# Splitting the last product's output over two PSUM banks, two loads made of three, and one zero product fewer, in a decode kernel of attention and MLP

## The chip, the cores and the metric

The kernel runs on one core of one Trainium2 chip. The metric is the device time of one execution in microseconds (us). Six executions of the kernel before in the first comparison took 661.54 to 661.99 us. With one core there is no second die to compare with; all runs told of here are of state fast. The span in a profile (660.1 us) runs from the first to the last instruction and is about 1.4 us shorter than the time.

## The reference

Four tokens (batch 4, one position each, model width 640) pass a pre-norm attention block over a cache of 4096 positions with 32 heads, and then a pre-norm MLP with mish activation. Shapes and the part that matters:

```python
q = (layernorm(x) @ wq)                      # 640 -> 32 heads x 128
p = softmax(q . k_cache * 128**-0.5)         # k_cache 4 x 32 x 4096 x 128, bf16
h = x + (p . v_cache) @ wo                   # wo 4096 x 640
a = mish(layernorm(h) @ w1 + b1)             # w1 640 x 1728
out = h + a @ w2                             # w2 1728 x 640, out 4 x 1 x 640, bf16
```

The two caches are 268 MB of the 283 MB that are read. The change concerns the last few microseconds, `a @ w2 + h`, and the load of `wo`.

## The kernel before

Each engine has its own program; `need` waits for marks that other engines set. SyncE issues nearly all loads into one queue, in order: the caches, then `wo`, `w1`, `w2`. `w2` (13 full blocks of 128 rows, and a tail of 64) is loaded in row groups of 5, 4, 3 and 1 blocks, each with its own semaphore. The parts that the change touches (cuts marked):

```python
# N = 4 tokens, D = 640, KO = 2 halves of OC = 320 columns, QD = 32, FS = [0, 5, 9, 12, 13]
y2_ps = red[:, 0:KO, 0:OC]           # half k: PSUM bank k, partitions 32k to 32k + 3
WOS = [(k, 0, G) for k in range(NHG - 1)] + [(NHG - 1, a, b) for a, b in ((0, 4), (4, 7), (7, G))]

def store(p, h):                     # one half each: SyncE half 0, ScalarE half 1
    p.need(("o_bf", h))
    load(p, out_rows[:, h * OC : (h + 1) * OC], o_bf[h * QD : h * QD + N, :], ("out", h), f"OUT{h}")
# ScalarE, last:
ac.need(("y2", 1))
ac.do(lambda: a.copy(out=o_bf[QD : QD + N, :], in_=y2_ps[QD : QD + N, 1, :]), ("o_bf", 1), "AC")
store(ac, 1)
# VectorE, last:
dv.need(("y2", 0))
dv.do(lambda: v.tensor_copy(out=o_bf[0:N, :], in_=y2_ps[0:N, 0, :]), ("o_bf", 0), DV)

# TensorE, tail (cut): busy(n) issues n zero products of 512 columns into a bank that nobody reads
for c in range(DC):                  # the residual h, as products with an identity
    for k in range(KO):
        mm(y2_ps[k * QD : k * QD + N, k, :].rearrange("b (m c) -> b c m", c=DC)[:, c, :],
           st[:, c, :], ident_f[:, k * P // KO : (k + 1) * P // KO], False, False)
busy(4)
pe.need("act")
def w2_mm(j):                        # one block of rows: two products, in two column groups of the array
    for k in range(KO):
        mm(y2_ps[k * QD : k * QD + N, k, :], act[0:rows, j, :], ...)   # 4 x 320
pe.need("w2t"); w2_mm(FM)
for j0, j1 in zip(FS, FS[1:]):
    if j0 == FS[2]:
        busy(3)
    pe.need(("w2", j0))
    for j in range(j0, j1):
        w2_mm(j)
```

The softmax here doesn't subtract the row's maximum and nothing guards it: scores larger than these inputs give would overflow.

## Time and profile before

| what | value | where it is read |
|---|---|---|
| time | 661.62 us, median of 3 | the runs |
| DMA share | 9 tenths or more in 39 of 40 slices | page, part 2 |
| bytes read, rate | 283.35 MB, 429 GB/s | page, part 3 |
| TensorE, VectorE busy | 59%, 62% | page, part 1 |
| last wait for w1 | until 651.13 us | chain of waits |

The page of the kernel before; in the second line the engines' busy time in us, and in the digits one tenth per digit for 40 equal slices of the span:

```profile
span 660.1 us, 4898 instructions
...
PE 391.0 (59%) x2604; PEld 68.8 (10%) x1631; DVE 407.8 (62%) x255; ACT 41.1 (6%) x158; POOL 1.8 (0%) x13
...
DMA  9999999999999999999999999999999999999997
...
HBM read 283.35 MB, written 0.01 MB: 429 GB/s over the span
```

The load stream is the clock of this kernel. The two busiest engines are idle for some 40% of the span, and what they do is free as long as it ends before the next piece of data lands. Only after the last loads have landed does every instruction count. The chain of waits shows where that begins (start in us, duration, what):

```profile
627.60 23.53 DMA slotB<-in_B_w_dram
...
651.18 1.28 PE red L722 x29
...
655.10 1.68 PE red L722 x20
656.78 0.32 PE o_ps L722
...
657.54 0.69 PE red L722 x8
658.22 0.47 DVE o_bf L718
```

The long line is the wait for w1, 23.53 us from issue to landing. The tail after it is a chain of 9 us. The timeline of its end (start, duration, engine, line, operation, output and inputs, count, and in brackets the idle time before it and what ended it; PEld is a weight load):

```profile
655.10 0.30 PE L722 MATMUL red<-w_tail,act 64*4 64x320 bf16 x2 [0.22 <-DVE act L711]
...
655.33 1.46 PE L722 MATMUL red<-slotA,act 128*4 128x320 bf16 x18
656.07 0.36 PEld L722 LDWEIGHTS red<-slotA,act 128*4 128x4 bf16 x8 [0.25 <-DMA slotA<-in_B_w_dram]
...
656.71 0.39 PE L722 MATMUL o_ps<-zeros,ident 128*128 128x512 bf16 x1
656.94 0.60 PE L732 MATMUL o_ps<-zeros,ident 128*128 128x512 bf16 x2
657.47 0.36 PEld L722 LDWEIGHTS red<-slotA,act 128*4 128x4 bf16 x8 [0.66 <-DMA slotA<-in_B_w_dram]
657.47 0.71 PE L722 MATMUL red<-slotA,act 128*4 128x320 bf16 x8
658.21 0.48 DVE L718 CAST o_bf<-red 4x320 bf16<-4x320 f32 x1 [3.17 <-PE red L722]
658.25 0.42 ACT L441 CAST o_bf<-red 4x320 bf16<-4x320 f32 x1 [4.46 <-PE red L722]
658.69 0.28 ACTq L262 DMA_DIRECT2D out_dram<-o_bf  x1
658.72 0.35 SPq L262 DMA_DIRECT2D out_dram<-o_bf  x1
```

TensorE starts w2's second row group at 656.07, on the landing of its load. The three zero products (o_ps) follow, and the third and fourth group start at 657.47. "DMA" is named as the releaser there, but the trace has that load landed at 657.18: the zero products held it up. Then come two casts side by side, one on each engine, and two stores.

### The profile page before, as it was taken

To read this page: it belongs to the slowest core of one execution; us is meant where nothing else is said; L and a number is where in the kernel's file an instruction comes from. 1 tells how busy PE (TensorE), PEld (TensorE's weight loads), DVE (VectorE), ACT (ScalarE), POOL (GpSimd) and SP (SyncE) were. 2 spreads that over 40 slices of the span, in tenths; PEclk is the share of its full clock that TensorE was granted. 3 is DMA by queue.
4 is the path that set the end of the run, shared out by engine and by line. 5 is a ranking of instruction groups with operands and counts; after the bars stand their busy time and mean duration, and the time that the engine had idled before them with its cause. 6 is when DMAs were issued, how large, how long until landed. Compare 5 with 4: busy or idle time off the path is not lost. (4 is left out here: it accounts for less than half of the span.)

```text
span 660.1 us, 4898 instructions
## 1 busy us (share of the span) xinstructions
PE 391.0 (59%) x2604; PEld 68.8 (10%) x1631; DVE 407.8 (62%) x255; ACT 41.1 (6%) x158; POOL 1.8 (0%) x13
## 2 busy tenths in 40 slices
PE   1365758456327595838307485828534757675878
PEld 0100100101101010101100010100110001010145
DVE  1078988295048778677219688848306798867612
ACT  0200000000000000000000000000000000000011
POOL 0000000000000000000000000000000000000000
PEclk9999787879659796869668678977965879786869
DMA  9999999999999999999999999999999999999997
GB/s 417 409 445 445 438 441 417 422 445 438 434 437 425 429 445 433 437 437 425 429 445 433 437 437 425 429 445 433 433 445 425 425 445 433 433 445 425 413 419 308
DMA packets 6883, 283.48 MB, mean 429 GB/s; under 512 B 781, under 2 KB 1113, under 8 KB 2138
## 3 DMA queue, kind: packets, MB, share of 16 engines
q1 hardware_dynamic: 6856, 283.35, 99.4%
q8 instruction: 6, 0.10, 0.1%
q14 instruction: 3, 0.02, 0.0%
q10 hardware_dynamic: 18, 0.01, 0.0%
HBM read 283.35 MB, written 0.01 MB: 429 GB/s over the span
## 5 line engine op out<-in xcount | busy, mean ns | idle before, releaser
L529 DVE TENSOR_TENSOR slotA<-slotA,q_bc 128x8192 bf16<-128x8192 bf16 x32 | 140.6, 4415 | 90.5 <-DMA slotA<-in_A_k_cache_dram 90.5
L529 DVE TENSOR_TENSOR slotB<-slotB,q_bc 128x8192 bf16<-128x8192 bf16 x32 | 140.7, 4416 | 16.5 <-DMA slotB<-in_A_k_cache_dram 16.5
L540 DVE TENSOR_REDUCE s_f<-red 128x64 f32<-128x1024 f32 x64 | 78.0, 1218 | 98.5 <-PE red L732 98.4
L732 PE MATMUL red<-slotA,ident 128*128 128x512 bf16 x480 | 137.5, 450 | 0.0
L732 PE MATMUL red<-slotB,ident 128*128 128x512 bf16 x480 | 127.3, 425 | 0.0
L722 PE MATMUL red<-slotA,ident 128*128 128x512 bf16 x32 | 14.2, 445 | 126.4 <-PEq L49 126.4
L722 PE MATMUL pv<-slotC,e 128*32 128x512 bf16 x768 | 53.1, 437 | 36.8 <-PEq L49 33.9
L722 PE MATMUL red<-slotB,ident 128*128 128x512 bf16 x32 | 14.1, 441 | 87.2 <-PEq L49 87.2
L402 ACT ACTIVATE ex<-s_f 128x64 bf16<-128x64 f32 x64 | 16.4, 256 | 512.0 <-DVE s_f L540 512.0
L554 DVE TENSOR_TENSOR e<-ex,hmask 128x512 bf16<-128x512 bf16 x64 | 39.8, 682 | 0.0
L722 PEld LDWEIGHTS pv<-slotC,e 128*32 128x32 bf16 x768 | 22.6, 108 | 95.7 <-issue 82.1
L722 PEld LDWEIGHTS red<-slotA,ident 128*128 128x128 bf16 x32 | 3.2, 99 | 195.1 <-issue 195.0
L722 PEld LDWEIGHTS red<-slotB,ident 128*128 128x128 bf16 x32 | 3.1, 98 | 169.2 <-issue 169.2
L722 PEld LDWEIGHTS o_ps<-pv_sb,selo 128*32 128x32 f32 x136 | 13.5, 109 | 65.1 <-issue 65.1
L722 PE MATMUL o_ps<-pv_sb,selo 128*32 128x128 f32 x136 | 18.0, 276 | 0.0
L722 PE MATMUL pv<-slotA,e 128*32 128x512 bf16 x256 | 14.5, 380 | 0.2 <-PEq L49 0.2
L412 ACT COPY pv_sb<-pv 128x512 f32<-128x512 f32 x16 | 9.4, 585 | 69.8 <-PE pv L722 69.8
L402 ACT ACTIVATION_READ_ACCUMULATOR ex<-s_f 128x1 f32 x64 | 11.9, 186 | 0.0
L722 PEld LDWEIGHTS pv<-slotA,e 128*32 128x32 bf16 x256 | 6.7, 97 | 23.4 <-issue 17.5
L519 DVE CAST b1T<-pv 128x13 bf16<-128x13 f32 x1 | 0.2, 173 | 14.0 <-PE pv L722 14.0
L579 DVE RECIPROCAL rl<-misc 32x1 f32<-32x1 f32 x4 | 0.6, 150 | 12.8 <-PE misc L722 12.8
L722 PE MATMUL red<-slotC,lnT 128*32 128x512 bf16 x40 | 4.5, 631 | 5.6 <-PEq L49 5.6
(105 smaller groups left out, 76.3 us busy)
## 6 DMA issues: line engine op xcount, KB each, us to landing
slotC<-in_A_v_cache_dram SPq DMA_DIRECT2D x2, 4096.0 KB, 39.0
slotC<-in_A_wq_dram SPq DMA_DIRECT2D x1, 5120.0 KB, 15.5
slotB<-in_A_wo_dram SPq DMA_DIRECT2D x3, 1280.0 KB, 15.6
slotB<-in_B_w_dram SPq DMA_DIRECT2D x2, 864.0 KB, 22.5
slotA<-in_B_w_dram SPq DMA_DIRECT2D x1, 800.0 KB, 18.5
slotB<-in_A_wo_dram SPq DMA_DIRECT2D x1, 640.0 KB, 19.3
slotA<-in_B_w_dram SPq DMA_DIRECT2D x1, 640.0 KB, 18.9
slotB<-in_A_wo_dram SPq DMA_DIRECT2D x1, 480.0 KB, 20.0
```

Of the source, the lines that this page charges most:

```text
L402: lambda: a.activation(out=ex[:, sl], in_=s_f[:, sl], func=ACT.Exp, scale=SCALE, accum_out=rs[:, b, s : s + 1],),
L412: lambda: a.copy(out=pv_sb[:, :, :].rearrange("p r d -> p (r d)"), in_=pv[:, :]),
L519: dv.do(lambda: v.tensor_copy(out=b1T[:, 0:FM], in_=b1_ps[:, 0:FM]), "b1m", DV)
L529: lambda: v.tensor_tensor(out=t, in0=t, in1=q_bc[:, hg, b, :].unsqueeze(1).to_broadcast([P, RS, Dh]), op=ALU.mult,),
L540: lambda: v.tensor_reduce(out=s_f[:, s * RS : (s + 1) * RS], in_=red[:, k : k + 2, :].rearrange("p k (r c) -> p (k r) c", c=CW), axis=AX.X ...
L554: lambda: v.tensor_tensor(out=e[:, sl, :], in0=ex[:, sl].unsqueeze(2).to_broadcast([P, RS, G]), in1=hmask[:, :].unsqueeze(1).to_broadcast( ...
L579: dv.do(lambda: v.reciprocal(out=rl[:, :], in_=l_ps), ("rl", hg), DV)
L722: lambda: nc.tensor.matmul(out_, lhsT=lhsT, rhs=rhs, start=start, stop=stop, skip_group_check=skip),
L732: return t.add_instruction(mybir.InstMatmult(name=nc.get_next_instruction_name(), engine=mybir.EngineType.PE, ins=[t.lower_ap(rhs), t.lowe ...
```

## The change

Its intent: each cast reads 160 columns instead of 320, so that both end sooner. For that each half is put in two banks, so that VectorE reads bank 0 and ScalarE bank 1 of both halves. (The Trainium skill, "PSUM — Partial Sum Buffer", section "PSUM bank collisions raise a hardware error", asks that two engines never be on one bank and quadrant at once; two banks keep to that.) As each half now comes from both engines, each store waits for both. Besides, one zero product goes, and wo's last row group is loaded in two parts, 5 and 3 rows per partition instead of 4, 3 and 1.

```diff
+    QC = OC // 2
+    y2_ps = red[:, 0:2, 0:QC]
-    ... for a, b in ((0, 4), (4, 7), (7, G))]
+    ... for a, b in ((0, 5), (5, G))]
     def store(p, h):
-        p.need(("o_bf", h))
+        p.need(("o_bf", 0), ("o_bf", 1))
-            a.copy(out=o_bf[QD : QD + N, :], in_=y2_ps[QD : QD + N, 1, :])
+            a.copy(out=o_bf[0 : QD + N, QC:OC], in_=y2_ps[0 : QD + N, 1, :])
-        v.tensor_copy(out=o_bf[0:N, :], in_=y2_ps[0:N, 0, :])
+        v.tensor_copy(out=o_bf[0 : QD + N, 0:QC], in_=y2_ps[0 : QD + N, 0, :])
-        for k, w in enumerate((OC, OC, 512, 512)):     # zeroing of the banks
+        for k, w in enumerate((QC, QC, 512, 512)):
     # residual: 20 products of 32 columns instead of 10 of 64 (cut)
     def w2_mm(j):
-            for k in range(KO): mm(y2_ps[k * QD : k * QD + N, k, :], ...)
+            last = j == FM - 1
+            order = [(h, q) for q in range(2) for h in range(KO)] if last else [
+                (h, q) for h in range(KO) for q in range(2)]
+            for h, q in order:         # half h, bank q, 160 columns
+                args = (y2_ps[h * QD : h * QD + N, q, :], act[0:rows, j, :], ...)
+                if last or q == 0: mm(*args)
+                else: mm_same(*args, tile=(rows, QD), place=(0, h * QD))   # no weight load
-                busy(3)
+                busy(2)
```

## The prediction

> **What bounds it now.** The page: DMA share 9 tenths in 39 of 40 slices, 429 GB/s, 283.35 MB in a span of 660.1 us; TensorE 59%, VectorE 62%. The kernel is a load stream with a short tail; the change touches only the tail.
>
> The chain of waits and the timeline give the tail. The second w1 part lands at 651.13 and TensorE starts on it at 651.18. w1 ends near 653.25, the activation at 655.05, w2 starts at 655.10. TensorE then waits for w2's second row group (landing 656.03, products from 656.07). They stream until 656.61, three zero products run 656.71 to 657.37, w2's third group starts at 657.47 although its data landed at 657.18. Products end at 658.18; VectorE casts 658.21 to 658.69 (479 ns), ScalarE 658.25 to 658.66 (416 ns); stores are issued at 658.69 and 658.72, and 1.37 us later the last lands.
>
> **What the change does, costed.**
> 1. One zero product fewer in the w2 tail: they step 0.22 us. The third group would start at 657.25; its landing (657.18 plus about 0.04) allows that, the last row (lands 657.57, wanted about 657.6) just about. Gain 0.2 us, on the chain.
> 2. Casts of 160 instead of 320 columns. Each engine casts one half before too, so its work only halves. From casts of 56 (192 ns) and 320 columns (479 ns) I estimate 305 ns on VectorE; for ScalarE, from copies of 512 (585 ns) and 320, 275 ns. 36 partitions instead of 4 should cost nothing. But each store now waits for both casts, and the second bank is ready 0.07 us after the first: ScalarE decides. Gain 0.15 us, on the chain.
> 3. wo's last group in two DMAs: packets of 5120, 3840, 1280 B (196, 149, 55 ns) become 6400 and 3840 (244, 149). Eight each per engine: every later landing comes 0.06 us earlier, and w1 and w2 wait for landings. Gain 0.05 us. The earlier issue gains nothing, the queue is backlogged.
> 4. Zero products for `red` 160 wide: 0.27 us of TensorE at 643.5, absorbed by the 1 us wait for w1 at 650.2.
> 5. Residual products, 20 to 40 passes of 32 columns: 0.56 us now, 0.6 to 0.9 then (the Trainium skill, "TensorE: Matmul & The Clock Gate", section "Back-to-back issue gap", states a floor of about 60 cycles for 1 to 64 columns; here pairs of 64-column fp32 passes step 56 ns). TensorE is 0.4 us ahead of the activation, plus 0.25 us before 656.03: absorbed.
> 6. w2: 26 products of 320 columns become 52 of 160. Pairs in the two column groups run side by side now, 135 ns per row. In the new order products sharing weights are in one column group, and only neighbours across groups overlap; if they do, a row takes 137 ns. If not, up to 270 ns: eight rows on the chain cost up to 1 us. This is the main risk.
>
> **Sum.** 0.2 + 0.15 + 0.05 = 0.4 us gain if 5 and 6 cost nothing; I leave a little for them. Predicted 661.3 us (before 661.62), range 660.8 to 661.8. Faster by over 2%: 0.003; within 2%: 0.994; slower: 0.003.
>
> **What would show it.** In the timeline: third w2 group starts near 657.25; casts near 0.3 us; both stores issued near 658.35, ScalarE's cast last; w1's second part lands near 651.07; w2 starts unchanged at 655.1; four w2 products step 137 ns.
>
> **What would make it wrong.** Same-group neighbours serialising (6); residual products or an added instruction fetch delaying w2; landings drifting by tenths between executions, as large as the effect itself (the three runs differ by 0.44 us).

## The result

The kernel after took 661.32 us (median of 6, 661.04 to 661.84), the kernel before 661.74 us (median of 6). The ratio is 0.9994 with a 95% interval of 0.9981 to 1.0007. A ratio is the mean time of one kernel's fast runs over that of the other's of the same rounds, so not quite the ratio of the medians. At 2% this is "same", and the interval contains 1. Below, differences of means are given too: here 661.34 less 661.74, or -0.39 us when taken before rounding.

The page after has the same limits:

```profile
span 660.1 us, 4968 instructions
...
PE 388.3 (59%) x2651; PEld 69.3 (11%) x1653; DVE 407.5 (62%) x255; ACT 40.9 (6%) x158; POOL 1.8 (0%) x13
...
DMA  9999999999999999999999999999999999999997
...
HBM read 283.35 MB, written 0.01 MB: 429 GB/s over the span
```

The chain of waits after; the same wait for w1 stands in it, and the cast at its end is now ScalarE's:

```profile
627.02 24.14 DMA slotB<-in_B_w_dram
...
651.21 1.29 PE red L726 x29
...
658.22 0.28 ACT o_bf L442
```

The timeline after, at the places shown of before:

```profile
655.37 0.24 PE L726 MATMUL red<-slotA,act 128*4 128x160 bf16 x2
655.44 0.24 PE L736 MATMUL red<-slotA,act 128*4 128x160 bf16 x2
655.51 0.24 PE L726 MATMUL red<-slotA,act 128*4 128x160 bf16 x2
...
656.27 0.44 PEld L726 LDWEIGHTS red<-slotA,act 128*4 128x4 bf16 x8 [0.32 <-DMA slotA<-in_B_w_dram]
...
656.93 0.39 PE L726 MATMUL o_ps<-zeros,ident 128*128 128x512 bf16 x1
657.15 0.38 PE L736 MATMUL o_ps<-zeros,ident 128*128 128x512 bf16 x1
657.46 0.51 PEld L726 LDWEIGHTS red<-slotA,act 128*4 128x4 bf16 x10 [0.44 <-DMA slotA<-in_B_w_dram]
...
657.88 0.31 PE L726 MATMUL red<-slotA,act 128*4 128x160 bf16 x4
658.15 0.32 DVE L720 CAST o_bf<-red 36x160 bf16<-36x160 f32 x1 [3.07 <-PE red L726]
658.22 0.28 ACT L442 CAST o_bf<-red 36x160 bf16<-36x160 f32 x1 [4.40 <-PE red L726]
658.59 0.35 SPq L263 DMA_DIRECT2D out_dram<-o_bf  x1
658.60 0.28 ACTq L263 DMA_DIRECT2D out_dram<-o_bf  x1
```

Both casts are shorter (0.32 and 0.28 us). Two zero products take the place of three, and w2's third group starts 1.19 us after the second (657.46 less 656.27), not 1.40. Yet the third group starts at the same time as before: in this execution the loads of w2 landed 0.2 us later. The span of this profile is 660.10 us against 660.12. So a profile's end tells little here. What can be read from one is a distance between two events. Three distances are used from here on, all in us:

- **landing**: from the landing of the last V piece to that of w2's second group (the load stream alone);
- **end**: from the start of w2's third group to the end of the span (products, casts, stores);
- **store**: from SyncE's store to its last landing.

They come from the trace's records of landings and starts, to a nanosecond.

| kernel | landing | second to third group | end | store |
|---|---|---|---|---|
| before | 21.755 | 1.395 | 2.650 | 1.366 |
| after | 21.816 | 1.190 | 2.633 | 1.471 |

The surprise is in the last two columns. The first store is issued 1.128 us after the third group's start and not 1.222, 0.094 us sooner. But the end comes only 0.017 us sooner (2.633 for 2.650): from the first store to the end it is now 1.505 us and was 1.428, and SyncE's store, whose landing is the last, takes 0.105 us longer. (Before, SyncE's store is the second of the two, 0.028 us after ScalarE's; after, it is the first, by 0.007 us. Counted from the first store to the last landing the difference is 0.077 us.)

### The profile page after: what moved, and what is told of

The parts are those of the page before. It is cut to its first block, busy times and chain, and to the rows that moved or that the text cites. A ratio compares the mean times of both kernels' runs of the same rounds, so it can differ in the third digit from the quotient of the medians.

```text
span 660.1 us, 4968 instructions
## 1 busy us (share of the span) xinstructions
PE 388.3 (59%) x2651; PEld 69.3 (11%) x1653; DVE 407.5 (62%) x255; ACT 40.9 (6%) x158; POOL 1.8 (0%) x13
## 5 line engine op out<-in xcount | busy, mean ns | idle before, releaser
L736 PE MATMUL red<-slotA,ident 128*128 128x512 bf16 x480 | 135.4, 445 | 0.0
L726 PE MATMUL red<-slotA,ident 128*128 128x512 bf16 x32 | 14.4, 449 | 127.0 <-PEq L49 127.0
```

Source lines behind the costliest of these rows:

```text
L726: lambda: nc.tensor.matmul(out_, lhsT=lhsT, rhs=rhs, start=start, stop=stop, skip_group_check=skip),
L736: return t.add_instruction(mybir.InstMatmult(name=nc.get_next_instruction_name(), engine=mybir.EngineType.PE, ins=[t.lower_ap(rhs), t.lowe ...
```

## The experiments

Twelve runs were made, all correct (e1 is the changed kernel again, e8 that of e2). The first four shared a chip and the runs of the kernel before, and so did the next four and the last four. The summary first; "difference" is the mean of the runs less the mean of the kernel before. Kernels are compared only within the same rounds.

| run | what | difference, us | ratio, 95% interval | landing | end | store |
|---|---|---|---|---|---|---|
| (first comparison) | the change | -0.39 | 0.9994 (0.9981 to 1.0007) | 21.816 | 2.633 | 1.471 |
| e1_again | the change | -0.32 | 0.9994 (0.998 to 1.0008) | 21.823 | 2.636 | 1.474 |
| e2_only_split | split alone | +0.11 | 1.0002 (0.9988 to 1.0015) | 21.930 | 2.634 | 1.474 |
| e8_split_again | split alone | +0.14 | 1.0002 (0.9989 to 1.0016) | 21.903 | 2.635 | 1.473 |
| e3_only_busy | one zero product fewer alone | -0.21 | 0.9997 (0.9983 to 1.001) | 21.808 | 2.657 | 1.374 |
| e4_only_wo | wo in two DMAs alone | -0.05 | 0.9999 (0.9985 to 1.0013) | 21.666 | 2.643 | 1.360 |
| e10_no_split | change without the split | -0.35 | 0.9995 (0.9981 to 1.0008) | 21.731 | 2.646 | 1.364 |
| e5_split_busy | change without the wo part | 0.00 | 1.0 (0.9987 to 1.0014) | 21.885 | 2.643 | 1.482 |
| e7_swap | change, waits swapped | -0.22 | 0.9996 (0.9983 to 1.001) | 21.758 | 2.595 | 1.470 |
| e9_both_wait | before, stores wait for both | -0.08 | 0.9997 (0.9982 to 1.0012) | 21.846 | 2.781 | 1.473 |
| e11_one_store | e10 with one store | -0.25 | 0.9996 (0.9982 to 1.0009) | 21.771 | 2.648 | one store, 1.295 |
| e6_pad | before, longer program | +0.03 | 0.9999 (0.9986 to 1.0013) | 22.006 | 2.645 | 1.364 |
| e12_no_split_pad | e10, longer program | -0.29 | 0.9995 (0.9981 to 1.0009) | 22.039 | 2.644 | 1.363 |

No interval excludes 1. The single executions of a kernel spread by 0.2 to 0.8 us, so a difference of 0.1 us between means of five is not told from none. What is shown below is shown by distances in traces, and times are used where they are 0.2 us or more.

### e1 to e4: the change again, and its parts one by one

**e1_again**: no edit.

> The changed kernel unaltered, for the size of the difference. Theory A (three small gains on the chain add up): 0.3 to 0.45 us faster than the kernel before, interval clear of zero. Rival B (the 0.42 us of the first comparison are drift of the landings): 0.0 to 0.15 us. In the profile, third w2 group to first store issue 1.14 us again (before: 1.22), and the stores issued with ScalarE's cast last.

It measured 661.24 us (661.15 to 661.54) against 661.63 us before. Third group to first store was 1.128 us, as expected 1.14. The difference of the first comparison came back at about the same size (-0.32 after -0.39). That speaks for Theory A and against drift, though the interval of the ratio alone does not decide it.

**e2_only_split**: the change with the other two parts undone.

```diff
-    ((0, 5), (5, G))
+    ((0, 4), (4, 7), (7, G))
-                busy(2)
+                busy(3)
```

> Only the split of each half over two banks and the two 160-column casts; three zero products and wo in three DMAs as before. Theory A: third w2 group to first store issue falls by 0.08 to 0.15 us, time 0.1 us faster. Rival C (the split alone carries the whole gain): 0.3 us or more faster. The third w2 group should start later than its landing plus 0.05, bound by the zero products.

It measured 661.69 us, no gain at all. The distance to the first store did fall by 0.095 us, as expected, but neither theory was right about the time.

**e3_only_busy**: the kernel before with `busy(2)` for `busy(3)`.

> Only the one zero product fewer in the w2 tail. Theory A: w2's third group starts 1.19 us after its second instead of 1.40 us, time 0.2 us faster. Rival D (the loads decide: the third group's landing comes so late that TensorE waits for it anyway): less than 0.1 us. Casts stay 0.48 and 0.42 us.

It measured 661.44 us, -0.21, and all five runs (661.28 to 661.53) lie at or below the lowest of the nine before (661.51), but for one at 661.53. The timeline of e3_only_busy around the zero products:

```profile
656.13 0.36 PEld L722 LDWEIGHTS red<-slotA,act 128*4 128x4 bf16 x8 [0.27 <-DMA slotA<-in_B_w_dram]
...
656.77 0.39 PE L722 MATMUL o_ps<-zeros,ident 128*128 128x512 bf16 x1
657.00 0.38 PE L732 MATMUL o_ps<-zeros,ident 128*128 128x512 bf16 x1
657.30 0.45 PEld L722 LDWEIGHTS red<-slotA,act 128*4 128x4 bf16 x8 [0.44 <-DMA slotA<-in_B_w_dram]
```

The third group starts 1.177 us after the second. Its load landed at 657.24 in this trace, 0.06 before the start: both limits meet here. From landing to start TensorE took 0.045 us at the second group before (656.029 to 656.074), so a further zero product taken away would gain an estimated 0.02 us. The zero product is worth its 0.2 us. A rival would be that TensorE, with less to do, is granted a slower clock; the traces before, after and of e3 show a granted clock of 1.00 in every stretch from 653 us to the last product.

**e4_only_wo**: the kernel before with `((0, 5), (5, G))`.

> Only wo's last row group in two DMAs. Theory A: the first w1 part lands 14.34 us after the last V piece instead of 14.40, and every later landing 0.06 us earlier with it; time 0.05 us faster, too little to be told from zero. Rival E (fewer DMAs issued earlier matter): 0.3 us or more.

It measured 661.58 us, -0.05. The first w1 part landed 14.331 us after the last V piece, against 14.394. That pair of traces alone proves nothing: over all fourteen traces this part lands at 14.40 us on average with two DMAs and with three. The gain stands in the later landings. The second w1 part, for which TensorE waits, lands at 16.667 to 16.881 us (mean 16.762) in the seven traces with two DMAs and at 16.858 to 16.938 (mean 16.897) in the seven with three, and w2's second group at 21.801 against 21.876 on average. Rival E (an earlier issue matters) falls. In the time the gain cannot be told from zero, as expected.

The two parts that gain, e3 and e4, sum to -0.26 us; the change has -0.32 and -0.39.

### e5, e8: what the split is worth beside the others

**e5_split_busy**: the change with `((0, 4), (4, 7), (7, G))` put back.

> Split and one zero product fewer, wo still in three DMAs. If the parts add as the traces' chains do (Theory A): 0.3 us faster than the kernel before. If the split gives nothing by itself, as its first run had it: 0.2 us, the same as the zero product alone. Third w2 group to first store issue 1.14 us, second to third group 1.19 us or the landing.

It measured 661.65 us, 0.00 us apart from before, 0.2 less than even the zero product alone gives. Its trace has every distance of the change (1.191 us from second to third group, end 2.643), so the tail explains no loss. The landing was 21.885. This run fits no sum of parts; with runs from 661.37 to 661.88 I leave it as unexplained.

**e8_split_again**: the kernel of e2 once more.

> The split alone once more, to see whether its zero is real. Theory A (its gain on the chain is real): 0.1 us faster than before; if the first run was typical: 0.0 to 0.1 us slower, with w2's second group again landing 21.9 us after the last V piece.

It measured 661.76 us, +0.14. Ten runs of the split alone now have no gain. Its landing, 21.903, was late again, as the expectation had it. In the two profiled executions of the split alone the later landing (0.175 and 0.148 us) accounts for the loss; the tail itself is 0.016 and 0.015 us shorter than before.

### e9: why the casts' gain is lost

**e9_both_wait**: the kernel before, its casts untouched.

```diff
-        p.need(("o_bf", h))
+        p.need(("o_bf", 0), ("o_bf", 1))
```

> The kernel before, with one edit: each of the two stores waits for both casts, as the split makes them. Theory S (two stores issued at the same instant, 0.01 us apart, are handled interleaved and end later than two issued 0.03 us apart): SP's store to its last landing rises from 1.37 to about 1.47 us and the packets of the two queues interleave, though the casts are the old ones. Rival T (it is the split data, written by two engines over 36 partitions): stays 1.37 us.

What Theory S foretold came, and Rival T falls. The timeline of e9_both_wait:

```profile
658.58 0.48 DVE L718 CAST o_bf<-red 4x320 bf16<-4x320 f32 x1 [3.17 <-PE red L722]
658.61 0.42 ACT L441 CAST o_bf<-red 4x320 bf16<-4x320 f32 x1 [4.46 <-PE red L722]
659.11 0.35 SPq L262 DMA_DIRECT2D out_dram<-o_bf  x1
659.12 0.27 ACTq L262 DMA_DIRECT2D out_dram<-o_bf  x1
```

The casts are those of before (0.48 and 0.42 us, 4 partitions, one engine each). What differs is that SyncE's store comes 0.008 us before ScalarE's, where before ScalarE's came 0.028 us ahead. The store's last landing then takes 1.473 us, as in the kernels with the split (1.470 to 1.482), and not 1.366. The packets tell a part of it. Before, the four 640-byte packets of ScalarE's queue start in even steps of about 0.026 us, and SyncE's four follow 0.1 us behind in the same steps. In e9, as in the change, the steps are uneven and both rows stretch: ScalarE's fourth packet starts 0.152 us after its first, not 0.078, and SyncE's 0.137, not 0.078. That is 0.059 of the 0.107 us; from the start of SyncE's last packet to the landing it takes another 0.068 longer, and its first packet comes 0.020 sooner after the store's issue. What inside the queues' hardware does it is not shown. Nor is the closeness of the stores told from their order: the edit brought them together and put SyncE's first, and no run has one without the other.

A second cost comes on top. Before, each store starts 0.03 us after its own cast (ScalarE's cast ends at 658.66, the store is at 658.69). In e9 the first store is issued 0.055 us after the later cast, and in the change 0.083 us (the next experiment tells why).

So the waits and the meeting of the stores cost 0.131 us by themselves (end 2.781, before 2.650): 0.053 us up to the first store (1.275 for 1.222) and 0.078 us from there to the end (1.506 for 1.428). The split's shorter casts give back 0.146 (2.781 to 2.635 in e8): the later cast ends 0.174 us sooner after the third group's start (1.046 for 1.220), and 0.027 of that go to a longer step from the cast to the store. What the split is worth is the rest, 0.015 us. These are distances in one trace each; in the time of e9 no loss shows (-0.08 us over four runs).

### e7: the order of the two waits

**e7_swap**: the change with one line altered.

```diff
-        p.need(("o_bf", 0), ("o_bf", 1))
+        p.need(("o_bf", 1), ("o_bf", 0))
```

> The changed kernel with the two waits of each store in the other order, so that the store itself waits for ScalarE, which ends last, and VectorE's wait stands apart ahead of it. Expected: ScalarE's cast end to first store issue 0.03 us instead of 0.09, time 0.05 us less than the change, 0.45 us faster than before. Rival: the step is the queue's own and stays 0.09.

In these traces a store carries one of its two waits, and the other is an instruction of its own ahead of it. In the change the store carried VectorE's wait and the separate one was ScalarE's, which ends last. (In e9 the store carried VectorE's too, and there VectorE ended last: 0.055 us.) The timeline of e7_swap:

```profile
658.16 0.29 ACT L442 CAST o_bf<-red 36x160 bf16<-36x160 f32 x1 [4.33 <-PE red L726]
658.49 0.35 SPq L263 DMA_DIRECT2D out_dram<-o_bf  x1
658.50 0.28 ACTq L263 DMA_DIRECT2D out_dram<-o_bf  x1
```

From the end of ScalarE's cast to the first store it is now 0.046 us, against 0.083: less gain than the expected 0.06, but the step is not the queue's own. One account fits all these numbers: in the eight traces with two waits SyncE's store is issued 0.081 to 0.083 us after the cast that the separate wait stands for, and ScalarE's 0.090 to 0.092. That cast is ScalarE's in e9 (659.027, store 659.109) and in the change (658.508, store 658.591), and VectorE's in e7 (658.405, store 658.488). The cast whose wait the store carries ended later in e9 and e7, and did not decide. With one wait, carried by the store, it took 0.03 us. So a separate wait costs some 0.05 us, and e7 only moved it to the cast that ends first. The end shrinks to 2.595. In the time (661.42 us, -0.22, where -0.45 was expected) this does not show.

### e10, e11: without the split, and with one store

**e10_no_split**: the kernel before with `busy(2)` and `((0, 5), (5, G))`.

> The change without the split: one zero product fewer and wo in two DMAs, casts and stores as before. If the split gains nothing (its casts' 0.1 us are given back by the stores): as fast as the change, 0.2 to 0.4 us faster than before. If the split is worth its 0.1 us: slower than the change by 0.1 us. First store issue to end of span 1.40 us, not 1.50.

It measured 661.45 us, -0.35, with all runs from 661.23 to 661.53 against 661.51 to 662.10 before. So two edits of one line each gain what the whole change gains. The timeline of e10_no_split:

```profile
657.29 0.71 PE L722 MATMUL red<-slotA,act 128*4 128x320 bf16 x8
658.03 0.48 DVE L718 CAST o_bf<-red 4x320 bf16<-4x320 f32 x1 [2.97 <-PE red L722]
658.07 0.42 ACT L441 CAST o_bf<-red 4x320 bf16<-4x320 f32 x1 [4.27 <-PE red L722]
658.51 0.28 ACTq L262 DMA_DIRECT2D out_dram<-o_bf  x1
658.54 0.35 SPq L262 DMA_DIRECT2D out_dram<-o_bf  x1
```

The old casts, the stores 0.026 us apart again, and 1.397 us from the last store to the end, where the change has 1.498.

**e11_one_store**: e10, with both casts writing into partitions 0 to 3 and one store from ScalarE.

```diff
-        p.need(("o_bf", h))
-        load(p, out_rows[:, h * OC : (h + 1) * OC], o_bf[h * QD : h * QD + N, :], ...)
+        p.need(("o_bf", 1), ("o_bf", 0))
+        load(p, out_rows[:, :], o_bf[0:N, :], ...)       # ScalarE only
-    a.copy(out=o_bf[QD : QD + N, :], ...)
+    a.copy(out=o_bf[0:N, OC:D], ...)
```

> The last one, with both casts writing side by side into four partitions and one store of 4 x 1280 bytes from ScalarE's queue in place of two. Theory S: the store no longer shares the queues' time: cast end to store 0.03 us, store to landing 1.2 to 1.3 us, end 0.1 to 0.15 us earlier than the last one; 0.35 to 0.5 us faster than before. If a store of twice the bytes takes as much longer: no gain over the last one.

This missed. It measured 661.54 us, 0.1 more than e10. Its store was issued 0.092 us after the later cast, which here was VectorE's (658.645, ScalarE's 658.614), while the store carried ScalarE's wait; and one store of twice the bytes landed after 1.295 us, not the 1.206 of ScalarE's small one. The end was 2.648, as in e10 (2.646). No version that clearly beats the change was found.

### e6, e12: a longer program

The traces with the split had late landings of w2 (21.758 to 21.930, mean 21.852 of six) beside the short, unsplit ones (21.666 to 21.846, mean 21.763 of six), though the loads are the same. The changed kernel has 70 instructions more (4968 for 4898 in the profiles), and one more instruction fetch of 16 KB (at 657.16 us in the trace after, none there before).

**e6_pad**: the kernel before with products added behind the last one, where nothing waits.

```diff
+        for k in range(69):
+            (mm_same if k else mm)(o_full[:, 0:1], ident[:, :], zeros[:, :], True, True)
```

> The kernel before with 69 one-column products and one weight load added behind the last w2 product, where nothing waits for them: the program is as much longer as the split makes it, and nothing else differs. Theory F (a longer instruction stream, with a third instruction fetch in the tail, makes the w2 loads land later, which ate the split's gain): w2's second group lands 21.87 to 21.93 us after the last V piece, not 21.73 to 21.81, and the time is 0.1 to 0.15 us longer. Rival G (the later landings in the three traces with the split are drift): landing and time as before, within 0.05 us.

**e12_no_split_pad**: the same addition in e10.

> The change without the split, with the 69 padding products of the earlier padded run behind the last w2 product. Theory F (a longer program moves the w2 landings): in this profile w2's second group lands 0.1 to 0.3 us later after the last V piece than in the run without padding, and the time is 0.1 us longer or more, as TensorE now waits for these landings. Rival G (drift): landing and time within 0.07 us of that run.

In both traces the landing moved, to 22.006 and 22.039: 0.25 us later than before and 0.31 later than e10, more than Theory F had foretold. The queue lines of the page name the extra fetch, here for e10_no_split:

```profile
q8 instruction: 6, 0.10, 0.1%
```

and here for e12_no_split_pad:

```profile
q8 instruction: 7, 0.11, 0.1%
```

But that seventh fetch starts at 659.03 us, after all loads have landed, so the fetch itself can't be the cause. And the times hardly moved: +0.03 us against before, and -0.29 where e10 had -0.35, neither told from zero. The profiled executions were longer (661.95 against 661.56 us, and 661.60 against 661.38), the others not. So that a longer program makes w2 land later rests on profiled executions, one of each padded kernel; both lie above the six short, unsplit ones. The traces show where much of the time goes: between 650 and 653 us the load packets take longer than at their best, which costs 0.41 to 0.45 us in the six short programs and 0.46 to 0.62 in the eight longer ones (summed, divided by 16 engines), most in the two padded. Why, and whether it costs anything in other executions, stays open. The spread of the runs does not decide it (standard deviations 0.14 to 0.29 us for the eight sets of long programs, 0.09 to 0.11 for e3, e4, e10 and e11, but 0.21 for e9 and 0.09 to 0.21 for the kernel before).

## Why the prediction was right or wrong

The total was right: 661.3 foretold, 661.32 measured. That they agree to 0.02 us is luck. One of the three terms was wrong. With the 0.015 us that the split is worth in the traces, the terms sum to an estimated 0.27 us (0.2 of e3, 0.05 of e4, and 0.015), not to 0.4, and the spread of the runs hid it. And "same" at 2% had to come out for any gain of this size.

1. *One zero product fewer, 0.2 us*: right. 1.190 us from second to third group instead of 1.395, and -0.21 us alone (e3). The start "near 657.25" was not seen, because that execution's load landed at 657.38; the distance was. Two more of the foretold times were missed: w1's second part landed at 651.16, not 651.07, and the stores came at 658.59, not 658.35, of which 0.21 us are the third group's later start.
2. *Shorter casts, 0.15 us net*: wrong. The durations were right (316 and 285 ns for 305 and 275 estimated; 36 partitions cost nothing), and so was "ScalarE's cast last". The step that failed is "each store now waits for both casts ... ScalarE decides", which was priced at 0.07 us for the second bank's delay and nothing else. It lacked two terms: 0.053 us until the first store, as the second wait is an instruction of its own (0.083 us from cast to store instead of 0.03), and 0.078 us from there to the end, as the two stores, released together, meet in the queues (or as SyncE's now goes first). e9 shows both without the split. The casts' 0.15 us is real against e9; net 0.015 us remain. I had taken "1.37 us later the last lands" as a constant; it was 1.47 us once the stores came together.
3. *wo in two DMAs, 0.05 us*: right as far as can be seen: the second w1 part lands 0.135 us sooner on average and w2's second group 0.075, time -0.05 (e4). "Every later landing" is too much: the first w1 part does not.
4. *Narrower zeroing, absorbed*: consistent. The two narrowed products take 0.15 us where they took 0.29, and TensorE waits for w1 until 651.21 after as before.
5. *Residual products, 0.6 to 0.9 us*: cheaper, 0.58 us, and absorbed as foretold: w2 starts at 655.14 (655.10 before). Pairs of passes step 0.029 us instead of 0.056. The floor that I cited (60 cycles, which the page puts at about 25 ns) did not bind: the pairs are 29 ns apart. Within a pair the two starts are only 7 ns apart; that they are in different column groups the trace does not say.
6. *Four products step 137 ns*: right, 138 ns. The risk of a serial order did not come true. How it came out is a surprise (last section).

The foretold extra instruction fetch came, at 657.16 us, where it delays nothing on the chain.

What is left open: why the stores take longer when released together, and why longer programs land later. The change has 0.06 to 0.13 us more than e3 and e4 together, which is within the noise, and e5 has 0.2 us less than its parts.

## What to carry to other kernels

When work is split over two engines to shorten it, ask what then starts at the same instant: here the casts gained 0.15 us, and the stores that had to wait for both, and met in the queues, gave 0.13 of it back. At an effect of 0.1 us in 660, compare distances inside the traces, and test each part alone: two one-line edits carried the whole gain. Where an instruction has two waits, let it carry the one that ends last, and let the separate one be for what ends early: here the step from its cast to the store was 0.08 to 0.09 us, and 0.03 with the carried one alone.

## What the Trainium skill lacked or had wrong

- "TensorE: Matmul & The Clock Gate", section "The mechanism", says that matmuls are "pc-monotone in start AND end — strict FIFO, no reordering". The records here, by the lines that the trace names, have another order of starts. A block of w2 has four products in program order: half 0 bank 0 (line 726), half 0 bank 1 (line 736), half 1 bank 0 (726), half 1 bank 1 (736). In the timeline after, both of line 726 start first (655.374 and 655.379 us), then both of line 736 (655.442 and 655.447). As I read it, a product for a free column group passed one that waited for its own. The 5 ns between the two of one line are near the 4 ns that the page gives for the issue of one tile more (section "Measured speedup vs the span model").
- "DMA: Bandwidth & Descriptors", section "Issuing engines are not separate DMA queues", says that DMAs issued by two engines run on the same DMA engines "and interleave with each other". In e9 and the change the packets of the two queues alternate, as it says; which DMA engines carry them the traces do not tell. The page lacks a price: two stores of 2.5 KB issued 0.008 us apart, SyncE's first, land 0.08 us later after the first of them than two issued 0.028 us apart, ScalarE's first (1.473 us in e9 and 1.394 before).
- "TensorEngine Tiling (Array Packing)", section "PSUM Bottleneck", advises to use both ScalarE and VectorE to evacuate PSUM. Both kernels do. Halving the columns per engine took 0.16 and 0.13 us off the casts, and 0.015 us off the end: the advice lacks that the join behind it costs.
- No page that was read for this gives the cost of a second wait on one instruction: in all eight traces with two waits the stores came 0.081 to 0.092 us after the cast that the separate wait stood for, and about 0.03 us after their own cast where they had one wait alone.
- No page has the slow stretch that begins at about 650.3 us in all these traces and lasts to 652.4 us or longer: packets of w2's first group (6400 bytes) take 0.244 us at best and up to 0.42 us before and 0.47 after, in which the load stream loses 0.41 to 0.62 us (the packets' time over their best, summed and divided by 16 engines). Packets of 6400 bytes of wo, at 644 us in the trace after, have 0.244. Its cause was not tested.
